# mLSTM cell in front of an MLP with a tanh-shrink, one core: the cell rebuilt with paired heads and a second part two slots behind its scores

## The chip, the core and the metric

The kernel runs on one core of a Trainium2 chip. The metric is the device time of one execution in microseconds (us), as the median of several runs. The core has five engines with an instruction queue each: PE (matrix multiplication, with its weight loads PEld), DVE (vector), ACT (scalar), POOL and SP, which here only issues DMAs. PE writes to PSUM, eight banks of 2 KB per partition; DVE and ACT read from it.

## What is computed

A recurrent cell over 4 batches, 8 heads, 768 tokens and 40 features per head, and behind it a dense part over all 3072 tokens (320 features, 2048 hidden). All of it in fp32.

```python
for t in range(S):
    m_new = np.maximum(f_gate[:, :, t] + m, i_gate[:, :, t])
    f_stab = np.exp(f_gate[:, :, t] + m - m_new)
    i_stab = np.exp(i_gate[:, :, t] - m_new)
    C = f_stab * C + i_stab * outer(vt, kt)      # 40 x 40 per head
    n = f_stab * n + i_stab * kt
    y[:, :, t] = sigmoid(o_gate) * (C @ qt) / np.maximum(np.abs(n @ qt), 1.0)
x = y, tokens by heads * features
h = x @ w_in
out = (h - np.tanh(h)) @ w_out
```

The weights arrive as 64-bit floats and are converted to fp32 in the kernel.

## The kernel before

**Cell.** The tokens are cut into 24 units of 128 tokens: unit n is chunk c = n // 4 of batch b = n % 4. Within a unit the recurrence is a product with a 128 x 128 decay matrix E per head, which one DVE scan (L321) makes from the gate's rows; across chunks a state of 40 x 41 per head goes on (the 41st column is n). A unit has these parts. `load_unit` (L132) issues five loads on SP's queue. `cell_open` (L311) issues the loads of E and qg, the scan on DVE, and on POOL the products qg (L324), vw (L326, L327) and vs (L330). `scores` (L332) multiplies k and q head by head (tile ps), four heads to a PSUM bank, and DVE multiplies four heads of E with it (L344). `output` (L364) adds, per head, state times qg and E times vw into the tile ph; its `close` divides and gates: den on DVE (L389 to L391), o times den on POOL (L392), ys on DVE (L394). `carry` (L348) makes pc, eight products of k and vs, and adds it to the state on DVE (L358) after POOL has decayed the state (L357). `turn` (L398) transposes ys into px, and ACT copies it to xT (L408). The tiles ph, pc and px share the two PSUM banks of the pool ps_b; ps has the two banks of ps_a.

A slot k (`cell_slot`, L413) is the list of steps: load unit k + 1, scores of the first four heads of unit k, turn of unit k - 2, output of unit k - 1, scores of the last four heads of unit k, carry of unit k - 1.

**Dense part.** Two units make a group of 256 tokens, twelve groups in all. An item is one group with one of eight pairs of 128-row blocks of the hidden layer: `up` (L433) makes 128 x 2 x 256 values in ph_up with 6 products, ACT and DVE compute h - tanh(h) from it in nine operations (L451 to L459) to the tile gt, and `down` (L463) adds 4 products into po, two items later. Each fp32 product of the program stands as two MATMUL instructions with a weight load each in the trace.

**Weights.** `weights` (L233) fetches a block as 64-bit integers and takes it apart on DVE (L255, L258), ACT (L256, L259, L260), POOL (L261, L262) and DVE again (`sign`, L266). `convert` strings blocks together so that each step fetches one block, computes the magnitude of another and the sign of a third.

**Order.** PE's instructions run in the order in which they are emitted (each hangs on the last, L75). The other engines' queues are ordered by a scheduler at compile time, which may draw ready instructions forward: the scans of units 16 to 18 start at 254.8, 267.3 and 298.0 us, before their slots. Slots 0 to 3 run ahead of the dense part, mixed with the conversion of pairs 0 and 1. The first six groups then go through the pairs in three passes (0 and 1; 2 to 4; 5 to 7), since the weights of later pairs are converted meanwhile; the other six groups go through all eight pairs. Slots 4 to 15 are spread over the twelve items of the first pass, one to an item; the last ten slots over the items from the second of the third pass on. Within an item `merge` (L492) alternates dense steps and cell steps by their written costs:

```python
            i = int(done[1] / total[1] < done[0] / total[0])
            if at[i] == len((a, b)[i]):
                i = 1 - i
            cost, step = (a, b)[i][at[i]]
            done[i] += cost
            at[i] += 1
            step()
```

Of the kernel before, what the change touches and what calls it, by code (L numbers as in the profile page):

```python
# [28 lines left out]
FP = mybir.dt.float32  # L30
# [22 lines left out]
def kernel(  # L53
# [71 lines left out]
    qk = [{name: const.tile([128, H, L], FP, name=f"{name}{i}") for name in ("qT", "kT")} for i in range(2)]  # L125
    for pair in qk:
        for name in pair:
            V.memset(pair[name], 0.0)
# [17 lines left out]
    ones = const.tile([128, D], FP, name="ones")  # L146
    diag = const.tile([128, H, L], FP, name="diag")
# [18 lines left out]
    eT = const.tile([D, NT, BH], FP, name="eT")  # L166
# [18 lines left out]
    for dst, w in ((eS, after), (eT, ones)):  # L185
        p = ps_b.tile([dst.shape[0], NT, BH], FP, name="psum_lf", tag="b")
        T.matmul(p.rearrange("p c n -> p (c n)"), w, lfT.rearrange("p c n -> p (c n)"),
                 start=True, stop=True)
        A.activation(out=dst, in_=p, func=AF.Exp)
# [32 lines left out]
    def spread(dst, rows, c, b):  # L222
        i, r = divmod((c * B + b) * H, NR)
        nc.sync.dma_start(out=dst, in_=rows[i:i + 1, r:r + H, :].to_broadcast([dst.shape[0], H, L]))
# [8 lines left out]
    def weights(dst, src):  # L233
# [4 lines left out]
        def fetch():  # L238
# [3 lines left out]
            w["st"] = conv.tile([128, n], I64, name="w64", tag="w64", bufs=4)[0:p]  # L242
            nc.sync.dma_start(out=w["st"], in_=src)

        def magnitude():
# [6 lines left out]
            r = w["r"] = conv.tile([128, n], I32, name="w_r", tag="w_r", bufs=3)[0:p]  # L252
# [20 lines left out]
    def convert(pairs):  # L273
# [9 lines left out]
        for x in range(len(blocks) + 3):  # L283
            def step(x=x):
                for late, part in enumerate((0, None, 1, 2)):
# [9 lines left out]
    qg = [const.tile([128, H, L], FP, name=f"qg{i}") for i in range(2)]  # L295
    ys = [const.tile([L, NK * 128], FP, name=f"ys{i}") for i in range(2)]
    state = [const.tile([128, H, D1], FP, name=f"state{b}") for b in range(B)]
    for i in range(2):
        G.memset(qg[i], 0.0)
        G.memset(ys[i], 0.0)  # L300
    for b in range(B):
        G.memset(state[b], 0.0)

# [4 lines left out]
    def per_token(t, w, k):  # L308
        return w[:, t["c"], t["hs"]].unsqueeze(2).to_broadcast([w.shape[0], H, k])

    def cell_open(n):  # L311
        c, b = divmod(n, B)
        t = un[n] = ld.pop(n)
        t["c"], t["b"], t["hs"] = c, b, slice(b * H, (b + 1) * H)
        E = t["E"] = att.tile([L, H, L], FP, name="E", tag="E", bufs=4)
        spread(E, f_rows, c, b)
        if c:
            t["qg"] = qg[n % 2]
            spread(t["qg"][0:D], g_rows, c, b)
        row = E.rearrange("p h t -> p (h t)")  # L320
        V.tensor_tensor_scan(out=row, data0=row, data1=diag.rearrange("p h t -> p (h t)"), initial=0.0,  # L321
                             op0=OP.mult, op1=OP.add)
        if c:
            G.tensor_tensor(out=t["qg"][0:D], in0=t["qg"][0:D], in1=t["qT"][0:D], op=OP.mult)  # L324
        vw = t["vw"] = att.tile([L, H, D1], FP, name="vw", tag="vw")
        G.tensor_tensor(out=vw[:, :, 0:D], in0=t["v"], in1=per_token(t, eiT, D), op=OP.mult)  # L326
        G.tensor_copy(out=vw[:, :, D], in_=eiT[:, c, t["hs"]])  # L327
        if c + 1 < NT:
            t["vs"] = att.tile([L, H, D1], FP, name="vs", tag="vs")
            G.tensor_tensor(out=t["vs"], in0=vw, in1=per_token(t, eS, D1), op=OP.mult)  # L330
# [256 lines left out]
```

## Time and profile before

| what | value |
|---|---|
| median of 3 runs (lowest, highest) | 742.69 us (741.7, 745.46) |
| the profiled execution | 744.64 us, span of the profile 742.9 us |
| PE, PEld busy | 668.3 us (90%), 542.9 us (73%) |
| DVE, ACT, POOL busy | 533.2 us (72%), 303.0 us (41%), 211.1 us (28%) |
| mean granted clock of PE | 0.924 |
| read from HBM, written | 46.20 MB, 4.13 MB |

The profile is of one execution. Busy is the time in which an engine ran instructions; a busy PE may run at half its clock. The granted clock is the share of full speed (2.4 GHz) that PE was given; it has two levels, 1.0 and 0.5, and a mean between them says how long each held. A row of the timeline or of the groups names line, engine, operation and "tile written <- tiles read"; brackets and the part behind a bar tell how long the engine idled before, and what ended that.

### The profile page before, as it was taken

What the parts mean: (1) busy time and instruction counts of PE and PEld (TensorE: products, weight loads), DVE (VectorE), ACT (ScalarE), POOL (GpSimd) and SP (SyncE); (2) the same over time, 40 slices, a digit from 0 to 9 for tenths busy, and PEclk for the clock granted to TensorE, in tenths of its full rate; (3) what the DMA queues carried; (4) which work ended last, traced back from release to release, by engine and by line L of the source; (5) the groups of instructions that cost most, each with busy time, mean ns of one, the idle gap of its engine ahead of it and who ended that gap; (6) DMA issues with size and microseconds to landing.
All of it is one profiled execution on the core that took longest, in us unless ns stands there. A gap on an engine that the chain in (4) does not pass through costs nothing.

```text
span 742.9 us, 9560 instructions
## 1 busy us (share of the span) xinstructions
PE 668.3 (90%) x3418; PEld 542.9 (73%) x3418; DVE 533.2 (72%) x845; ACT 303.0 (41%) x582; POOL 211.1 (28%) x226
## 2 busy tenths in 40 slices
PE   2477579898989977899999999999999999999997
PEld 1466468787877855678887877777778888877885
DVE  8775875786857898987768676766766665666665
ACT  3331332433422556644434343433354434544453
POOL 6385464644746456500021202020202020000000
PEclk9685896977869988999999999999999999999999
DMA  6562524444324612100011212120200100000000
GB/s 178 175 181 84 146 90 135 134 137 124 100 83 123 192 66 74 33 1 0 1 61 56 83 36 91 54 73 1 91 0 21 35 10 18 1 14 5 2 19 18
DMA packets 26487, 50.95 MB, mean 69 GB/s; under 512 B 3304, under 2 KB 15976, under 8 KB 26440
## 3 DMA queue, kind: packets, MB, share of 16 engines
q1 hardware_dynamic: 22568, 46.21, 20.0%
q10 hardware_dynamic: 3872, 4.13, 1.6%
q8 instruction: 27, 0.44, 0.2%
q14 instruction: 20, 0.16, 0.1%
HBM read 46.20 MB, written 4.13 MB: 68 GB/s over the span
## 4 chain that ended last, share of the span: by engine, by line
PE 67%; DVE 16%; POOL 9%; issue 5%; ACT 2%; ACTq 0%; DVEq 0%; POOLq 0%
PE ph_up L83 30%; PE po L83 23%; PE ph L83 8%; PE ps L83 4%; DVE E L321 3%; POOL w_r L261 3%; POOL w_r L262 2%; DVE gt L458 2%; PE pc L83 2%; DVE gt L457 2%; DVE gt L459 1%; POOL o L392 1%; DVE gt L455 1%; DVE t L456 1%; DVE w_e L255 1%
## 5 line engine op out<-in xcount | busy, mean ns | idle before, releaser
L83 PE MATMUL ph_up<-xT,w_in 128*128 128x256 f32 x1152 | 310.7, 397 | 0.0
L83 PE MATMUL po<-w_out,gt 128*128 128x320 f32 x768 | 253.5, 456 | 13.0 <-DVE part L477 6.6
L83 PEld LDWEIGHTS ph_up<-xT,w_in 128*128 128x128 f32 x1152 | 209.8, 195 | 32.4 <-issue 0.6
L83 PEld LDWEIGHTS po<-w_out,gt 128*128 128x128 f32 x768 | 140.9, 197 | 54.4 <-DVE part L477 8.7
L451 ACT ACTIVATE z<-ph_up 128x512 f32<-128x512 f32 x96 | 57.1, 595 | 263.4 <-PE ph_up L83 255.6
L455 DVE SCALAR_TENSOR_TENSOR gt<-ph_up,z 128x512 f32<-128x512 f32 x96 | 65.8, 685 | 98.6 <-ACT t L452 98.3
L83 PE MATMUL ps<-qT,kT 128*128 128x128 f32 x384 | 71.3, 313 | 27.2 <-DVE E L344 27.2
L83 PEld LDWEIGHTS ps<-qT,kT 128*128 128x128 f32 x384 | 68.0, 224 | 37.9 <-DVE E L344 28.6
L459 DVE COPY_PREDICATED gt<-big,t 128x512 f32<-128x512 int32 x96 | 81.3, 847 | 6.2
L83 PE MATMUL ph<-vw,E 128*128 128x41 f32 x384 | 80.2, 311 | 0.0
L457 DVE SCALAR_TENSOR_TENSOR gt<-z,gt 128x512 f32<-128x512 f32 x96 | 79.0, 823 | 0.0
L83 PEld LDWEIGHTS ph<-state,qg 128*128 128x128 f32 x320 | 64.9, 214 | 17.9 <-issue 7.4
L458 DVE SCALAR_TENSOR_TENSOR gt<-q,gt 128x512 f32<-128x512 f32 x96 | 72.1, 751 | 5.5
L453 ACT ACTIVATE q<-z,square 128x512 f32<-128x512 f32 x96 | 69.3, 722 | 0.0
L454 ACT ACTIVATE big<-z,border 128x512 f32<-128x512 f32 x96 | 69.1, 720 | 0.0
L357 POOL TENSOR_TENSOR state<-state,eT 40x328 f32<-40x328 f32 x16 | 11.9, 744 | 194.1 <-PE ph L83 194.1
L83 PEld LDWEIGHTS ph<-vw,E 128*128 128x128 f32 x384 | 66.1, 223 | 0.4 <-issue 0.2
L456 DVE TENSOR_TENSOR t<-ph_up,t 128x512 f32<-128x512 f32 x96 | 65.2, 679 | 0.0
L83 PE MATMUL ph<-state,qg 128*128 128x41 f32 x320 | 58.3, 268 | 5.6 <-DVE state L358 5.5
L261 POOL TENSOR_TENSOR w_r<-w_r,w_m 128x256 f32<-128x256 f32 (+2 forms) x40 | 39.1, 978 | 71.4 <-ACT w_m L259 65.7
L321 DVE TENSOR_TENSOR_SCAN E<-E,diag 128x1024 f32<-128x1024 f32 x24 | 59.0, 2456 | 0.0
L452 ACT ACTIVATE t<-ph_up 128x512 f32<-128x512 f32 x96 | 56.8, 592 | 0.0
(82 smaller groups left out, 488.4 us busy)
## 6 DMA issues: line engine op xcount, KB each, us to landing
E<-f_rows SPq DMA_DIRECT2D x24, 512.0 KB
w<-in_moe_w_out SPq DMA_DIRECT2D x16, 320.0 KB
w<-in_moe_w_in SPq DMA_DIRECT2D x16, 256.0 KB
qT<-in_qT SPq DMA_DIRECT2D x24, 160.0 KB
kT<-in_kT SPq DMA_DIRECT2D x24, 160.0 KB
v<-in_v SPq DMA_DIRECT2D x24, 160.0 KB
k<-in_k SPq DMA_DIRECT2D x24, 160.0 KB
o<-in_o_gate SPq DMA_DIRECT2D x24, 160.0 KB
```

The source lines that it names most:

```text
L83: return cls.keep(nc.tensor.matmul(*args, **kwargs))
L261: G.tensor_tensor(out=rf, in0=rf, in1=mf, op=OP.add)
L321: V.tensor_tensor_scan(out=row, data0=row, data1=diag.rearrange("p h t -> p (h t)"), initial=0.0, op0=OP.mult, op1=OP.add)
L451: A.activation(out=z, in_=ph, func=AF.Square)
L452: A.activation(out=t, in_=ph, func=AF.Tanh)
L453: A.activation(out=q, in_=z, func=AF.Square, bias=square)
L454: A.activation(out=big, in_=z, func=AF.Relu, bias=border)
L455: V.scalar_tensor_tensor(out=gt, in0=ph, scalar=lead, in1=z, op0=OP.mult, op1=OP.mult)
L456: V.tensor_tensor(out=t, in0=ph, in1=t, op=OP.subtract)
L457: V.scalar_tensor_tensor(out=gt, in0=z, scalar=root, in1=gt, op0=OP.add, op1=OP.mult)
L458: V.scalar_tensor_tensor(out=gt, in0=q, scalar=rest, in1=gt, op0=OP.add, op1=OP.mult)
L459: V.copy_predicated(gt, big.bitcast(I32), t)
```

## The change

The cell is written anew. Heads h and h + 4 form a pair. q2 holds both heads of a pair in one column block, the first at partitions 0 to 39, the second at 64 to 103; kz holds k the same way with zeros in the other half, so that a score still takes one product per head. The state of a pair is block-diagonal (104 partitions, 2 x 41 columns), so one product of qg and state serves two heads (`inter`), and so does one product of kp and vs (`update`), of which only the diagonal blocks are used. Each batch has two sets of states, and POOL writes the decayed old set into the new one. v1 carries a column of ones, so that vw and vs are one product each, vs with the factor eiS made once.

`fetch` loads unit s + 1 and its E in slot s; `decay` issues qg's loads and the scan of unit s; `prepare` runs POOL's products and the sigmoid of unit s - 1. The output of a unit is two slots behind its scores, its turn three, and within a slot scores, inter, intra and update alternate. The multiplication of o by den moves from POOL to DVE (`gate`). There are 27 slots: 0 to 3 ahead of the dense part, 4 to 16 in the first pass, 17 to 26 later, up to four items earlier than before. The conversion has one step more between magnitude and sign, and a buffer more for each of its two tiles.

```diff
--- before.py
+++ after.py
-    qk = [{name: const.tile([128, H, L], FP, name=f"{name}{i}") for name in ("qT", "kT")} for i in range(2)]
...
+    SEC = 64
+    TOP = SEC + D
+    kz = [const.tile([128, H, L], FP, name=f"kz{i}") for i in range(2)]
+    q2 = [const.tile([128, HH, L], FP, name=f"q2{i}") for i in range(2)]
+    kp = [const.tile([L, HH, TOP], FP, name=f"kp{i}") for i in range(4)]
+    v1 = [const.tile([L, H, D1], FP, name=f"v1{i}") for i in range(3)]
...
     def load_unit(n):
         c, b = divmod(n, B)
-        t = ld[n] = dict(qk[n % 2])
-        for name, src in (("qT", qT), ("kT", kT)):
-            nc.sync.dma_start(out=t[name][0:D], in_=src[b, c])
-        for name, src, bufs in (("v", v, 2), ("k", k, 3), ("o", o_gate, 3)):
-            t[name] = load.tile([L, H, D], FP, name=name, tag=name, bufs=bufs)
-            nc.sync.dma_start(out=t[name], in_=src[b, c])
+        t = ld[n] = {"kz": kz[n % 2], "q2": q2[n % 2], "kp": kp[n % 4], "v1": v1[n % 3]}
+        for half, (r0, h0) in enumerate(((0, 0), (SEC, HH))):
+            heads = slice(h0, h0 + HH)
+            nc.sync.dma_start(out=t["kz"][r0:r0 + D, heads], in_=kT[b, c, :, heads])
+            nc.sync.dma_start(out=t["q2"][r0:r0 + D], in_=qT[b, c, :, heads])
+        nc.sync.dma_start(out=t["v1"][:, :, 0:D], in_=v[b, c])
+        for r0, h0 in ((0, 0), (SEC, HH)):
+            nc.sync.dma_start(out=t["kp"][:, :, r0:r0 + D], in_=k[b, c, :, h0:h0 + HH])
+        t["o"] = load.tile([L, H, D], FP, name="o", tag="o", bufs=4)
+        nc.sync.dma_start(out=t["o"], in_=o_gate[b, c])
...
-    diag = const.tile([128, H, L], FP, name="diag")
+    diag = const.tile([128, H, L], BF, name="diag")
...
+    V.tensor_tensor(out=eiS, in0=eiT, in1=eS, op=OP.mult)
...
-            w["st"] = conv.tile([128, n], I64, name="w64", tag="w64", bufs=4)[0:p]
+            w["st"] = conv.tile([128, n], I64, name="w64", tag="w64", bufs=5)[0:p]
...
-            r = w["r"] = conv.tile([128, n], I32, name="w_r", tag="w_r", bufs=3)[0:p]
+            r = w["r"] = conv.tile([128, n], I32, name="w_r", tag="w_r", bufs=4)[0:p]
...
-                for late, part in enumerate((0, None, 1, 2)):
+                for late, part in enumerate((0, None, 1, None, 2)):
...
+    qg = [const.tile([128, HH, L], FP, name=f"qg{i}") for i in range(3)]
     ys = [const.tile([L, NK * 128], FP, name=f"ys{i}") for i in range(2)]
-    state = [const.tile([128, H, D1], FP, name=f"state{b}") for b in range(B)]
...
+    state = [[const.tile([128, HH, 2, D1], FP, name=f"state{b}_{i}") for i in range(2)] for b in range(B)]
+    for t in xT + qg + ys + sum(state, []):
+        G.memset(t, 0.0)
...
+    def fetch(n):
+        load_unit(n)
+        t = ld[n]
+        t["E"] = att.tile([L, H, L], FP, name="E", tag="E", bufs=4)
+        spread(t["E"], f_rows, n, 0)
+
+    def decay(n):
         t = un[n] = ld.pop(n)
...
+        if t["c"]:
+            t["qg"] = qg[n % 3]
+            for r0, h0 in ((0, 0), (SEC, HH)):
+                spread(t["qg"][r0:r0 + D], g_rows, n, h0)
+        row = t["E"].rearrange("p h t -> p (h t)")
         V.tensor_tensor_scan(out=row, data0=row, data1=diag.rearrange("p h t -> p (h t)"), initial=0.0,
                              op0=OP.mult, op1=OP.add)
...
+        t["vw"] = att.tile([L, H, D1], FP, name="vw", tag="vw", bufs=3)
+        G.tensor_tensor(out=t["vw"], in0=t["v1"], in1=per_token(eiT), op=OP.mult)
+        if t["c"]:
+            G.tensor_tensor(out=t["qg"][0:TOP], in0=t["qg"][0:TOP], in1=t["q2"][0:TOP], op=OP.mult)
+        if t["c"] + 1 < NT:
+            t["vs"] = att.tile([L, H, D1], FP, name="vs", tag="vs", bufs=3)
+            G.tensor_tensor(out=t["vs"], in0=t["v1"], in1=per_token(eiS), op=OP.mult)
...
+                G.tensor_tensor(out=new, in0=old, in1=eT[:, n, :].unsqueeze(2).to_broadcast([TOP, HH, 2 * D1]),
+                                op=OP.mult)
+        A.activation(out=t["o"], in_=t["o"], func=AF.Sigmoid)
...
+        T.matmul(t["ps"][:, h % HH, :], t["kz"][:, h, :], t["q2"][:, h % HH, :], start=True, stop=True)
...
+            T.matmul(pair(t["ph"], j), t["qg"][:, j, :], state[t["b"]][t["c"] % 2][:, j], start=(j == 0), stop=False,
+                     skip_group_check=True)
...
+        V.tensor_tensor(out=sg, in0=sg, in1=den.unsqueeze(2).to_broadcast([L, H, D]), op=OP.mult)
...
+        T.matmul(t["pc"][:, j], t["kp"][:, j, :], pair(t["vs"], j), start=True, stop=True)
...
+        for i, r0 in enumerate((0, SEC)):
+            new, pc = st[r0:r0 + D, :, i, :], t["pc"][r0:r0 + D, :, i, :]
+            if t["c"]:
+                V.tensor_tensor(out=new, in0=new, in1=pc, op=OP.add)
...
+    def cell_slot(s, o, x):
...
+        def begin():
+            if o is not None:
+                prepare(o)
+            if s is not None and s - 1 in un:
+                prepare(s - 1)
+            if s is not None:
+                if s + 1 < NU:
+                    fetch(s + 1)
+                decay(s)
+
+        steps.append((0.0, begin))
+        for d in range(HH):
+            for i in range(2):
+                if s is not None:
+                    steps.append((0.22, lambda h=2 * d + i: score(s, h)))
+                if o is not None and i == 0:
+                    steps.append((0.22 if o >= B else 0.0, lambda d=d: inter(o, d)))
+            if o is not None:
+                steps += [(0.22, lambda h=h: intra(o, h)) for h in (d, d + HH)]
+                if d in (1, 2) and o + B < NU:
+                    steps += [(0.18, lambda j=j: update(o, j)) for j in (2 * d - 2, 2 * d - 1)]
+        if o is not None:
+            steps.append((0.0, lambda: gate(o)))
+        if x is not None:
+            steps += [(0.11, lambda j=j: turn(x, j)) for j in range(NK)]
...
+    slots = [(0, None, None), (1, 0, None), (2, 1, 0), (3, None, 1)]
+    AHEAD = len(slots)
+    slots += [tuple(n if lo <= n < NU else None for n, lo in ((s, 0), (s - 2, 2), (s - 3, 2)))
+              for s in range(AHEAD, NU + 3)]
...
+    def slots_for(g):
+
+        return AHEAD if g == 0 else GT * g + 5
...
-    x0, x1 = starts[1, PASSES[-1][0]], starts[NG - 1, 0]
...
+    x0, x1 = starts[1, PASSES[-1][0]], starts[NG - 1, 0] - HH
```

## Rows read from the trace of the kernel before

**Rows 1.** Stages: stretch, its us; busy by engine; PEclk, DMA share, GB/s.

```profile
52.35:250.06 197.71, 166.90 (x1014) 143.59 (x1013) 141.10 (x212) 62.73 (x134) 103.83 (x108) 0.79 0.40 122
250.06:367.43 117.37, 106.10 (x423) 82.47 (x421) 98.14 (x163) 64.78 (x129) 37.74 (x33) 0.94 0.13 43
367.43:666.79 299.36, 298.02 (x1505) 237.34 (x1503) 204.92 (x320) 121.80 (x219) 37.86 (x38) 1.00 0.12 39
```

**Rows 2.** Same view, single items of the first pass.

```profile
192.17:203.54 11.37, 11.37 (x89) 10.10 (x87) 8.95 (x16) 5.89 (x13) 6.39 (x8) 1.00 0.42 131
203.54:226.41 22.87, 19.32 (x88) 16.31 (x87) 13.81 (x21) 4.51 (x9) 11.74 (x13) 0.63 0.24 76
```

**Rows 3.** Timeline of one slow item: start, us, engine, line [idle before].

```profile
201.55 2.35 POOL L324 TENSOR_TENSOR qg<-qg,qT 40x1024 f32<-40x1024 f32 x1
...
201.70 2.75 DVE L457 SCALAR_TENSOR_TENSOR gt<-z,gt 128x512 f32<-128x512 f32 x1
...
207.14 0.49 DVE L394 TENSOR_TENSOR ys<-ph,o 128x320 f32<-128x320 f32 x1 [1.43 <-POOL o L392]
...
207.78 0.52 PE L87 MATMUL px<-ident,ys 128*128 128x128 f32 x3 [2.32 <-DVE ys L394]
```

**Rows 4.** Waits from 52 to 250 us: total, times, longest.

```profile
DVE den L389 <- PE ph L83: 33.0, 9, 7.0
...
PE ps L83 <- DVE E L344: 16.9, 3, 9.0
...
DVE w_out L266 <- POOL w_r L262: 8.4, 7, 2.4
...
DVE ys L394 <- POOL o L392: 6.6, 9, 1.4
```

**Rows 5.** Timeline of warm small matmuls, then two pieces of the chain.

```profile
75.93 0.30 PEld L83 LDWEIGHTS ph<-state,qg 128*128 128x128 f32 x2
...
76.38 0.30 PEld L83 LDWEIGHTS ph<-state,qg 128*128 128x128 f32 x2
...
79.47 0.97 PEld L83 LDWEIGHTS ps<-qT,kT 128*128 128x128 f32 x8
...
81.00 0.81 PE L83 MATMUL pc<-vs,k 128*40 128x41 f32 x16
...
320.16 2.59 PE ph_up L83 x12
...
322.75 2.15 PE po L83 x8
```

**Rows 6.** Groups from 52 to 250 us: busy us, mean ns | idle.

```profile
L321 DVE TENSOR_TENSOR_SCAN E<-E,diag 128x1024 f32<-128x1024 f32 x13 | 33.9, 2606 | 0.0
...
L457 DVE SCALAR_TENSOR_TENSOR gt<-z,gt 128x512 f32<-128x512 f32 x12 | 17.3, 1441 | 0.0
...
L456 DVE TENSOR_TENSOR t<-ph_up,t 128x512 f32<-128x512 f32 x12 | 8.1, 679 | 0.0
...
L394 DVE TENSOR_TENSOR ys<-ph,o 128x320 f32<-128x320 f32 x12 | 5.9, 488 | 6.6 <-POOL o L392 6.6
...
L324 POOL TENSOR_TENSOR qg<-qg,qT 40x1024 f32<-40x1024 f32 x12 | 29.1, 2422 | 3.9 <-DMA qg<-g_rows 3.9
...
L392 POOL TENSOR_TENSOR o<-o,den 128x320 f32<-128x320 f32 x12 | 10.5, 878 | 3.8 <-DVE den L391 3.8
```

**Rows 7.** DMA queues (packets, MB, share), and one issue by SP.

```profile
q1 hardware_dynamic: 22568, 46.21, 20.0%
q10 hardware_dynamic: 3872, 4.13, 1.6%
175.65 0.38 SPq L139 DMA_DIRECT2D v<-in_v  x1
```

**Rows 8.** POOL: a memset's group, and the first conversion's row.

```profile
L231 POOL MEMSET w_in<- 128x2048 f32 x1 | 1.8, 1804 | 0.0
...
21.01 0.72 POOL L261 TENSOR_TENSOR w_r<-w_r,w_m 128x256 f32<-128x256 f32 x1 [5.67 <-ACT w_r L260]
```

More of the change, by code (lines that the diff above doesn't have):

```diff
@@ L122 @@
     nc.sync.dma_start(out=i_sb, in_=i_gate)
-    qk = [{name: const.tile([128, H, L], FP, name=f"{name}{i}") for name in ("qT", "kT")} for i in range(2)]
-    for pair in qk:
-        for name in pair:
-            V.memset(pair[name], 0.0)
+    SEC = 64
[4 more added lines that the diff above has]
+    v1 = [const.tile([L, H, D1], FP, name=f"v1{i}") for i in range(3)]
+    for i in range(4):
+        if i < 2:
+            V.memset(kz[i], 0.0)
+            V.memset(q2[i], 0.0)
+        V.memset(kp[i][:, :, D:SEC], 0.0)
+        if i < 3:
+            V.memset(v1[i][:, :, D:D1], 1.0)
     ld = {}
@@ L332, in scores @@
-    def scores(n, half):
-        h4 = slice(half * HH, (half + 1) * HH)
-        def product(j):
-            if j == 0 and half == 0:
-                cell_open(n)
-            t = un[n]
-            if j == 0:
-                t["ps"] = ps_a.tile([L, HH, L], FP, name="ps", tag="a")
-            h = half * HH + j
-            T.matmul(t["ps"][:, j, :], t["kT"][:, h, :], t["qT"][:, h, :], start=True, stop=True)
-            if j == HH - 1:
-                V.tensor_tensor(out=t["E"][:, h4, :], in0=t["ps"], in1=t["E"][:, h4, :], op=OP.mult)
-        return [(0.22, lambda j=j: product(j)) for j in range(HH)]
@@ L348, in carry @@
-    def carry(n):
-        def update(h):
-            t = un[n]
-            st = state[t["b"]]
-            if h == 0:
-                t["pc"] = ps_b.tile([D, H, D1], FP, name="pc", tag="b")
-            T.matmul(t["pc"][:, h, :], t["k"][:, h, :], t["vs"][:, h, :], start=True, stop=True)
-            if h == H - 1:
-                if t["c"]:
-                    G.tensor_tensor(out=st[0:D], in0=st[0:D], in1=per_token(t, eT, D1), op=OP.mult)
-                    V.tensor_tensor(out=st[0:D], in0=st[0:D], in1=t["pc"], op=OP.add)
-                else:
-                    V.tensor_copy(out=st[0:D], in_=t["pc"])
-        return [(0.08, lambda h=h: update(h)) for h in range(H)] if n // B + 1 < NT else []
@@ new lines, in intra, with gate @@
+    def intra(n, h):
+        t = un[n]
+        T.matmul(t["ph"][:, h, :], t["E"][:, h, :], t["vw"][:, h, :], start=(t["c"] == 0 and h == 0), stop=True,
+                 skip_group_check=True)
+    def gate(n):
+        t = un[n]
+        ph, sg = t["ph"], t["o"]
+        den = att.tile([L, H], FP, name="den", tag="den")
+        V.tensor_scalar(out=den, in0=ph[:, :, D], scalar1=-1.0, scalar2=1.0, op0=OP.mult, op1=OP.max)
+        V.tensor_tensor(out=den, in0=den, in1=ph[:, :, D], op=OP.max)
+        V.reciprocal(out=den, in_=den)
+        V.tensor_tensor(out=sg, in0=sg, in1=den.unsqueeze(2).to_broadcast([L, H, D]), op=OP.mult)
+        y = t["y"] = ys[n % 2]
+        V.tensor_tensor(out=y[:, 0:DM].rearrange("p (h d) -> p h d", d=D), in0=ph[:, :, 0:D], in1=sg, op=OP.mult)
```

163 lines of the change are left out of this document (69 added, 94 removed).

## The prediction, written before the changed kernel had been run

> **What bounds the kernel now.** Four views, in this order. The stage table first [rows 1]: after a prologue, the stretch from 52 to 250 us, in which twelve items of the dense part carry twelve cell slots, has a granted clock of 0.79, PE busy 84% and DVE busy 71%. Nothing is full there. From 250 to 367 us DVE is busy 84% (weights are still converted), and from 367 to 667 us PE is busy 99.6% at clock 1.00: that stage is bound by PE's instructions and by nothing else.
>
> Then the same stretch cut at the first matmul of each item [rows 2]. The twelve rows fall into two kinds, and one of each stands there: six of 9.2 to 12.2 us with clock 1.00 (mean 11.4) and six of 18.8 to 23.4 us with clock 0.59 to 0.77 (mean 21.6). A slow item does the same work; its PE is cold and idle. So 6 x 10.2 = 61 us of the 198 us are the price of the slow items.
>
> Third, one slow item's start in the timeline [rows 3]. POOL multiplies qg for 2.35 us; DVE's L457, issued 0.15 us later, takes 2.75 us and ends 0.55 us after POOL; ys waits 1.43 us for POOL's o; PE's transposes wait 2.32 us for ys, because px, ph and pc share two PSUM banks. After the stall follows the output phase, 32 matmuls of 41 columns. That item is the slow one of [rows 2], clock 0.63.
>
> Fourth, the waits of the stretch [rows 4]: DVE waits 33.0 us at den for PE's ph, and 15.0 us for POOL (w_out 8.4, ys 6.6); PE waits 16.9 us for the decay product E.
>
> **PE's instructions, part by part.** Warm, two small matmuls of ph follow two others every 0.22 us (the pair of state at 75.93, that of vw, the next of state at 76.38), so one costs 0.11 us [rows 5]; it is not the 41 columns, since pc has as many on 40-column weights at 0.05; a score costs the same (8 in 0.97 us, 0.12). What counts is the number of 128-column weight loads. The dense item costs 2.59 + 2.15 = 4.74 us [rows 5].
> - State times qg: 16 instructions per unit become 8 of 82 columns, still bound by the load: -8 x 0.11 = -0.88 us for each of 20 units.
> - pc: 16 in 0.81 us [rows 5], 0.05 each with 40-column weights; now 8 with 104-column weights. Bounds 0.05 and 0.11 each, so 0.4 to 0.9 us; nearest to 128 columns, I take 0.09, 0.7 us: no change.
> - Scores, the product with vw and the transposes keep their counts. Alternating the kinds buys nothing by itself, since 0.11 is the price in a run of one kind and in a mixture.
> - One slot more lies in the first pass (slots 4 to 16, thirteen, were 4 to 15), one fewer behind: its scores, 16 x 0.11 = 1.8 us of PE, move forward.
>
> **DVE, POOL, ACT, SP.** DVE's 141.1 us in the stretch [rows 1] change thus. The gating of sg comes over from POOL: nearest is ys, same shape, 0.49 us [rows 6], 13 times, +6.4. The state's addition is split by partitions: 679 ns for 512 columns and 488 for 320 [rows 6] give 1 ns a column, so 0.50 us for 328 and 2 x 0.33 for twice 164, +0.16 x 11 = +1.8. The slot moved forward brings a scan and two products of 512 columns, 2.6 + 2 x 0.68 = +4.0. The bf16 diag I price at nothing (bounds: nothing, or half of each scan, -17 us; the count of elements is unchanged). Blocking: L457 costs 1441 ns against 679 for L456 of the same shape, 9.1 us in the stretch, and the scan 2606 [rows 6]. POOL's work falls by half of qg's 2.42 us (half the columns) and by o's 0.88 [rows 6], 2.1 us a unit, 25 of the 104 us of [rows 1]; I take a third off those 9.1, -3 (bounds 0 and -9). Together 150.3 us, 12.5 per item; PE warm needs 4.74 + 13/12 x 40 x 0.11 + 0.8 + 0.4 = 10.7. So with no wait at all DVE becomes the bound of this stretch, at 150 us.
>
> Sigmoid only moves earlier on ACT, which is busy 62.7 us of 198 [rows 1]: nothing. POOL's memsets grow by some 6,200 columns, 5.5 us at w_in's 1.80 us for 2048; POOL idles 5.67 us before its first w_r [rows 8]: covered, and without that cover the first weights would be late by them. The conversion's last step comes one step later with one more buffer: DVE's 8.4 us of waits for w_r [rows 4] should go.
>
> SP issues 11 loads a unit for 7, at 0.38 us [rows 7] 4.2 us plus about 0.6 for weights; if an issue grows with its runs (1024 for v, 512 twice for k, against 128), 3.0 + 3.0 + 8 x 0.38 + 0.6 = 9.6 us. Both stay under 12.5. E, so far issued in the slot that scans it, is now issued one slot ahead, behind q2 and kz, which wait for POOL's qg of the unit before: a late POOL would hold E, then the scan, then the scores' bank; a slot of slack lies between.
>
> The data engines: v and k arrive in 2048 runs of 160 bytes a unit instead of 256 of 1280. The trace has no such run. Below, the bytes are the same: nothing. Above, the packets of the output queue (1067 bytes on average) took 0.016 x 16 x 742.9 / 3872 = 49 ns, those of the load queue (2048 bytes) 105 ns [rows 7]; at 49 ns each engine gets 128 x 0.049 - 1.0 = +5.3 us a unit on 0.40 x 198 / 12 = 6.6 us an item [rows 1], 12.3: just hidden. I take it as hidden. The Trainium skill (DMA: Bandwidth & Descriptors, Specifications) speaks against this part: under 512 bytes a transfer is read, modified and written, below line rate. By that, counted as two passes of the 49 ns, an item would have 19 us of transfers and the sum would come to 759 us, an estimate; no run here shows such a transfer.
>
> **The sum.** First stretch: 150.3 plus what remains of waiting. The 15.0 us for POOL go; of the 33.0 us at den, which come from six cold output phases, I keep those of two to three cold items, 14 us. That is 164 for 198: -34 (bounds 150 and 198). Prologue: unit 2's output leaves it, 16 x 0.12 + 0.8, -3 (bounds +3, should E come late, and -6). 250 to 367 us: DVE-bound with the same work and less blocking, -3 (0 to -8). Then nine outputs at -0.8 each (one load in ten lies behind a dense matmul) and the slot's scores -1.8: -9 (0, if stalls eat it, to -10). Sum -49. The profiled execution took 744.64 us (span 742.9), 2 us above the median of 742.69; against the median 742.7 - 49 = 694.
>
> **The rivals.**
> - *The banks hold it.* ph, pc and px still share two banks, and gate is now five DVE operations at the end of the slot, in front of the next ph. If the next ph waits for it each time, that is 1.5 us (three operations of 8 columns at 0.18 by the same line, two of 0.49) and up to a whole scan of 2.6 us in front [rows 6], PE stalls as in [rows 3], and the items stay mixed at 198 / 12 = 16.5 us. Then only prologue, conversions and half of the last stage remain: 742.7 - 3 - 1 - 4 = 735. For it: px waits just so in [rows 3]. Against: gate has lost its hop over POOL, and pc's bank comes free mid-slot.
> - *All items warm.* Nothing stalls PE for long, the small matmuls lie between scores and dense ones, and DVE's 150 us stand: 694 - 14 = 680; with the better bounds of the other stages 671.
> - *Slower: the short runs bound the slot.* If a run of 160 bytes costs what a 2048-byte packet does, 105 ns, an engine gets 128 x 0.105 - 1.0 = +12.4 us a unit, 13/12 of that on 6.6 is 20 us an item, 241 in the stretch: +43, less 15 elsewhere, 771. It costs from 59 ns on (where an item passes 13.7 us) and turns the gain into a loss near 88. Against it: 49 ns for far larger packets.
> - *The clock does not follow the order.* Falls come from stalls alone and the interleaving changes nothing: between forecast and first rival, 710; its chance is within the forecast's.
>
> **How the numbers follow.** Forecast 0.60, all warm 0.18, banks 0.12, short runs 0.07, anything else 0.03. A measurement can tell about 0.5%, 3.7 us. Faster takes the first two and two thirds of the banks: 0.86; same 0.06; slower 0.08. The range goes from 662 (all warm with the bounds of prologue, conversion and perhaps a faster scan) to 732, close to the banks' case; it leaves out the short runs and about half of the banks.
>
> **What would show it.** Item by item, the stretch should have two or three items over 16 us in place of six, a clock near 0.93, and DVE busy above 85% of it; no wait of ys or w_out for POOL; L457 nearer 1.1 us; state instructions 160 for 320; the late stage full at clock 1.00 and 8 to 10 us shorter. Wrong, if PE waits for ys or gate in most slots, if the transfers' share passes 0.8, or if the scan waits for E.

## The result, and the profile after

The changed kernel takes 708.01 us (median of four runs, 705.85 to 709.64) against 744.08 for the kernel before on the same chip (741.7 to 746.6): a ratio of 0.951, 95% interval 0.947 to 0.956. Forecast were 694, with a range of 662 to 732. So it is faster, as expected, but by 36 us in place of 49, and three of the forecast's four stages came out far from it. The profiled execution after has a span of 706.6 us. The stage table, cut at the same places as [rows 1] (the first matmul of items 0, 12, 33 and 82):

```profile
0.00:60.98 60.98, 28.02 (x137) 26.76 (x137) 46.62 (x89) 17.35 (x36) 33.14 (x54) 0.72 0.59 159
60.98:238.62 177.64, 145.35 (x869) 127.71 (x870) 142.40 (x238) 62.80 (x136) 81.34 (x88) 0.87 0.51 142
238.62:354.80 116.18, 104.37 (x423) 80.94 (x422) 101.14 (x168) 67.25 (x134) 35.36 (x34) 0.96 0.14 39
354.80:631.15 276.35, 276.35 (x1378) 228.84 (x1377) 202.03 (x332) 120.81 (x217) 14.61 (x15) 1.00 0.13 38
```

| stretch | before, us | after, us | forecast | came |
|---|---|---|---|---|
| up to the first dense item | 52.35 | 60.98 | -3 | **+8.6** |
| first pass, 12 items | 197.7 | 177.6 | -34 | **-20.1** |
| conversions | 117.4 | 116.2 | -3 | -1.2 |
| late stage | 299.4 | 276.4 | -9 | **-23.0** |
| rest | 76.1 | 75.5 | 0 | -0.6 |
| sum | 742.9 | 706.6 | -49 | -36.3 |

Three rows of the same view for single items answer to [rows 2]. The two kinds are gone: the twelve items last 11.8 to 18.8 us, 14.8 on average, and a shorter item can have a lower mean clock than a longer one (0.87 beside 0.95).

```profile
106.68:121.02 14.34, 10.23 (x58) 8.85 (x59) 10.95 (x22) 3.73 (x9) 7.15 (x8) 0.88 0.46 131
142.07:153.85 11.78, 11.78 (x73) 10.59 (x72) 10.42 (x18) 5.02 (x12) 4.80 (x6) 0.87 0.55 135
170.95:184.70 13.75, 11.40 (x73) 9.63 (x71) 11.01 (x19) 5.84 (x13) 6.24 (x7) 0.95 0.40 99
```

The waits of the first pass after the change (total, times, longest), which answer to [rows 4]:

```profile
POOL state L369 <- DVE state L420: 38.0, 7, 6.5
...
PE px L89 <- DVE state L420: 23.5, 7, 5.3
...
DVE w_out L291 <- POOL w_r L287: 12.1, 7, 1.9
...
DVE w_in L291 <- POOL w_r L287: 8.3, 8, 1.6
...
PE px L89 <- DVE state L422: 2.4, 1, 2.4
```

DVE's 33.0 us at den and its 6.6 at ys are gone. The waits for w_r, which were to go with them, are not: w_out has 12.1 us where it had 8.4, and w_in 8.3 where it had 7.8. And a wait has come that no row of before has: px, whose bank is the one that pc leaves, waits for the addition that reads pc. One such place in the timeline (it answers to [rows 3]): the addition's second half stands behind an instruction of the dense part in DVE's queue, and PE and POOL both go on 0.14 us after its end. That px is not held by ph's bank is seen from the gate, which begins to read ph only at 184.88 us.

```profile
182.19 0.31 DVE L420 TENSOR_TENSOR state<-state,pc 40x164 f32<-40x164 f32 x1
182.42 0.68 DVE L495 SCALAR_TENSOR_TENSOR gt<-q,gt 128x512 f32<-128x512 f32 x1
...
183.13 0.33 DVE L420 TENSOR_TENSOR state<-state,pc 40x164 f32<-40x164 f32 x1
...
183.60 1.19 POOL L369 TENSOR_TENSOR state<-state,eT 104x328 f32<-104x328 f32 x1 [6.40 <-DVE state L420]
183.60 0.52 PE L89 MATMUL px<-ident,ys 128*128 128x128 f32 x3 [2.32 <-DVE state L420]
```

The groups of the first pass (busy us, mean ns | idle), beside [rows 6]: the scan costs 2320 ns for 2606, what was L457 costs 728 for 1441, qg, with half the columns, 1470 for 2422, while a sign of w_out, behind POOL, costs 1207 for 891.

```profile
L348 DVE TENSOR_TENSOR_SCAN E<-E,diag 128x1024 f32<-128x1024 f32 x13 | 30.2, 2320 | 0.0
...
L363 POOL TENSOR_TENSOR qg<-qg,q 104x512 f32<-104x512 f32 x12 | 17.6, 1470 | 0.3 <-DMA qg<-g_rows 0.3
...
L291 DVE SCALAR_TENSOR_TENSOR w_out<-w,w_r 128x320 int32<-128x320 int32 x8 | 9.7, 1207 | 12.1 <-POOL w_r L287 12.1
...
L494 DVE SCALAR_TENSOR_TENSOR gt<-z,gt 128x512 f32<-128x512 f32 x12 | 8.7, 728 | 0.0
```

The load queue of [rows 7] now has three times the packets for the same bytes:

```profile
q1 hardware_dynamic: 69360, 46.22, 23.8%
```

### The profile page after: what moved, and what is told of

Read it like the earlier page. It is cut to its first block, busy times and chain, and to the rows that moved or that the text cites. A ratio compares the mean times of both kernels' runs of the same rounds, so it can differ in the third digit from the quotient of the medians.

```text
span 706.6 us, 9050 instructions
## 1 busy us (share of the span) xinstructions
PE 625.3 (89%) x3098; PEld 520.4 (74%) x3098; DVE 541.0 (77%) x897; ACT 303.4 (43%) x584; POOL 164.5 (23%) x190
## 4 chain that ended last, share of the span: by engine, by line
PE 69%; DVE 16%; POOL 5%; ACT 4%; issue 4%; DMA 2%; SPq 1%; ACTq 0%; POOLq 0%; DVEq 0%
PE ph_up L85 31%; PE po L85 25%; PE ps L85 5%; PE ph L85 5%; DVE E L348 3%; POOL w_r L286 2%; POOL w_r L287 2%; PE pc L85 1%; DVE gt L495 1%; DVE gt L494 1%; DVE gt L492 1%; DVE t L493 1%; DVE w_in L291 1%; PE px L89 1%; DVE E L380 1%
## 5 line engine op out<-in xcount | busy, mean ns | idle before, releaser
L85 PE MATMUL po<-w_out,gt 128*128 128x320 f32 x768 | 249.1, 449 | 10.7 <-DVE part L514 9.8
L85 PEld LDWEIGHTS po<-w_out,gt 128*128 128x128 f32 x768 | 138.8, 195 | 49.7 <-DVE part L514 12.1
L85 PE MATMUL ps<-q,kz 128*128 128x128 f32 x384 | 85.0, 323 | 17.5 <-DVE E L380 11.7
L85 PEld LDWEIGHTS ps<-q,kz 128*128 128x128 f32 x384 | 74.3, 228 | 25.8 <-DVE E L380 11.9
L496 DVE COPY_PREDICATED gt<-big,t 128x512 f32<-128x512 int32 x96 | 76.5, 796 | 6.5 <-DVE gt L495 0.5
L85 PEld LDWEIGHTS ph<-vw,E 128*128 128x128 f32 x384 | 69.4, 214 | 7.9
L494 DVE SCALAR_TENSOR_TENSOR gt<-z,gt 128x512 f32<-128x512 f32 x96 | 67.5, 703 | 0.0
L85 PE MATMUL ph<-vw,E 128*128 128x41 f32 x384 | 61.9, 267 | 0.0
L363 POOL TENSOR_TENSOR qg<-qg,q 104x512 f32<-104x512 f32 x20 | 28.2, 1410 | 117.4 <-DMA qg<-g_rows 90.1
L286 POOL TENSOR_TENSOR w_r<-w_r,w_m 128x256 f32<-128x256 f32 (+2 forms) x40 | 36.3, 907 | 56.2 <-ACT w_m L284 43.1
L366 POOL TENSOR_TENSOR vs<-v,eiS 128x328 f32<-128x328 f32 x20 | 17.7, 884 | 108.8 <-PE pc L85 108.8
L89 PE MATMUL px<-ident,ys 128*128 128x128 f32 x72 | 17.0, 305 | 26.5 <-DVE state L420 23.5
```

The source lines that it names most:

```text
L85: return cls.keep(nc.tensor.matmul(*args, **kwargs))
L286: G.tensor_tensor(out=rf, in0=rf, in1=mf, op=OP.add)
L494: V.scalar_tensor_tensor(out=gt, in0=z, scalar=root, in1=gt, op0=OP.add, op1=OP.mult)
L496: V.copy_predicated(gt, big.bitcast(I32), t)
```

## The late stage: what a narrow weight tile costs among wide ones

PE is full in this stage in both kernels, so every microsecond is PE's. Fitting the 49 items' times beyond 4.74 us by their counts of small instructions gives, before, 0.12 for a score, 0.11 for either half of ph, and **0.213** for pc; after, 0.11 for all and 0.102 for pc. So pc fell from 80 x 0.213 = 17.0 to 40 x 0.102 = 4.1 us, the state's products from 144 x 0.111 to 72 x 0.112 (-7.9), the scores by one slot's 16 (-2.7). These make up the 23 us, which is nearly two thirds of the whole gain. The forecast had the second and the third and took pc for unchanged. Two kernels part the width of pc's weights from their number.

**The kernel before, with wide weights (e3).** Its pc products load 80 columns, their own head and the next:

```
-            T.matmul(t["pc"][:, h, :], t["k"][:, h, :], t["vs"][:, h, :], ...)
+            T.matmul(t["pc"][:, h, :], t["k"][:, h:h + 2, :].rearrange("p two d -> p (two d)"), t["vs"][:, h, :], ...)
```

> The kernel before, with pc's weights 80 columns wide: each product loads its own head and the next one, and the lower 40 rows of the result alone are used. The instruction count stays 16 a unit. Theory (the width of the load relative to its neighbours is what costs): pc falls from 0.213 to about 0.11 us an instruction in the late stage, 80 x 0.1 = 8 us there (299.4 to some 291), the whole from 744 to about 735. Rival (only count and columns matter; 0.05 us in a run of pc goes up towards 0.11 with the wider load): the late stage is the same or longer by up to 5 us, the whole 744 to 749.

**The changed kernel, with narrow weights (e2).**

```
-        T.matmul(t["pc"][:, j], t["kp"][:, j, :], pair(t["vs"], j), ...)
+        for i, r0 in enumerate((0, SEC)):
+            T.matmul(t["pc"][r0:r0 + D, j, i, :], t["kp"][:, j, r0:r0 + D], t["vs"][:, j + i * HH, :], ...)
```

> pc goes back to one product per head on a 40-column weight tile (16 instructions a unit for 8), all else as after the change. Theory (a 40-column weight load among 128-column ones costs a switch): the late stage grows from 276.4 us by 80 x 0.213 - 40 x 0.102 = 13 us to some 289, the whole from 708 to 720 or more, and pc costs about 0.2 us an instruction there. Rival A (only the number of loads counts, 0.11 each): +4.4 us, 712. Rival B (the price read in a run of pc alone, 0.05 each): 80 x 0.05 - 40 x 0.102 = 0, no change.

Measured: e3's late stage is 291.5 us for 299.4 (-7.8), but of the whole only 2.5 us are gone, short of the expected 735, with a ratio to the kernel before of 0.996 (0.992 to 0.9995; in the profiled execution its first pass was 8 us longer, for a reason that was not sought); e2's late stage is 280.35 for 276.35 (+4.0), the whole 711.3 us, ratio 0.956 (0.950 to 0.962). The stage rows of e2 and of e3:

```profile
349.70:630.05 280.35, 280.35 (x1418) 226.21 (x1417) 201.93 (x332) 121.01 (x217) 15.08 (x15) 1.00 0.13 38
```

```profile
376.06:667.59 291.53, 289.75 (x1505) 240.27 (x1504) 205.15 (x320) 122.01 (x219) 37.15 (x38) 1.00 0.13 40
```

In the late stage e3 confirms that the width counts, while e2 hits the number of rival A, and read per instruction the two do not agree: in e2 a narrow pc costs 0.10, as a wide one does. The timelines bring them together. Call a visit the pc instructions that stand together between dense products. Before (first fence) and in e3 (second), pairs of pc alternate with pairs of po:

```profile
391.11 0.27 PE L83 MATMUL pc<-vs,k 128*40 128x41 f32 x2
391.31 0.81 PE L83 MATMUL po<-w_out,gt 128*128 128x320 f32 x2
392.05 0.27 PE L83 MATMUL pc<-vs,k 128*40 128x41 f32 x2
```

```profile
399.64 0.27 PE L83 MATMUL pc<-vs,kw 128*80 128x41 f32 x2
399.74 0.79 PE L83 MATMUL po<-w_out,gt 128*128 128x320 f32 x2
400.36 0.27 PE L83 MATMUL pc<-vs,kw 128*80 128x41 f32 x2
```

From one pc to the next it is 0.94 us with 40 columns and 0.72 with 80, and 40 such visits times 0.2 are e3's 8 us. In e2 (first fence) a visit is four narrow instructions long, after the change (second) two wide ones:

```profile
360.25 0.79 PE L85 MATMUL po<-w_out,gt 128*128 128x320 f32 x2
360.97 0.28 PE L85 MATMUL pc<-vs,kp 128*40 128x41 f32 x4
361.17 0.81 PE L85 MATMUL po<-w_out,gt 128*128 128x320 f32 x2
361.82 0.59 PE L85 MATMUL ph_up<-xT,w_in 128*128 128x256 f32 x2
```

```profile
365.35 0.79 PE L85 MATMUL po<-w_out,gt 128*128 128x320 f32 x2
365.98 0.33 PE L85 MATMUL pc<-vs,kp 128*104 128x82 f32 x2
366.14 0.74 PE L85 MATMUL po<-w_out,gt 128*128 128x320 f32 x2
366.72 0.59 PE L85 MATMUL ph_up<-xT,w_in 128*128 128x256 f32 x2
```

The same stretch, po to ph_up, takes 1.57 us and 1.37; 20 visits times 0.2 are e2's 4.0 us. Against two wide instructions in the same place, a visit of two narrow ones costs 0.2 us more, and a visit of four narrow ones costs 0.2 more too. So **the price is 0.2 us for each visit of 40-column weights among 128-column ones**, not for each instruction, and [rows 5] could not show it, since there the sixteen stand in one run. By this count some 8 of pc's 12.9 us are the 40 narrow visits, and the rest, about 4.5, the forty instructions fewer. The Trainium skill (TensorEngine Tiling (Array Packing), Key Properties) has a rule that the forecast did not use: changing the tiling mode of the array drains it, where another tile of the same mode does not. These runs agree with it only if a 40-column load runs in such a mode and an 80-column one does not, which no row says, so why a visit costs 0.2 us is not shown; the size is these runs' own.

## The first pass: a ring of waits

DVE is busy 142.4 of 177.6 us (80%), PE 82%; neither is full. Seven kernels change one thing each in the changed kernel; the last column is the ratio to the kernel before (the change itself: 0.951, 0.947 to 0.956).

| kernel | first item at | first pass | conversions end at | ratio |
|---|---|---|---|---|
| the change | 60.98 | 177.6 | 354.8 | 0.951 |
| e1, pc earlier | 60.7 | 187.7 | 369.5 | 0.971 (0.967 to 0.976) |
| f1, ph copied out by ACT | 60.0 | 174.2 | 349.3 | 0.945 (0.942 to 0.949) |
| k1, state's product kept back | 61.0 | 179.2 | 355.4 | 0.954 (0.950 to 0.958) |
| g1, no alternation | 58.2 | 182.8 | 358.5 | 0.958 (0.955 to 0.961) |
| g2, gate's product on POOL | 60.0 | 182.2 | 357.2 | 0.951 (0.948 to 0.955) |
| g3, one slot's distance | 66.96 | 155.9 | 345.9 | 0.944 (0.940 to 0.947) |
| s1, v and kp loaded twice | 57.75 | 174.9 | 348.7 | 0.947 (0.944 to 0.950) |

**e1: pc earlier.** If px waits for the state's addition, an earlier pc should free the bank in time.

```
-                if d in (1, 2) and o + B < NU:
-                    steps += [(0.18, lambda j=j: update(o, j)) for j in (2 * d - 2, 2 * d - 1)]
+                u = d - (o < AHEAD - 2)
+                if u in (0, 1) and o + B < NU:
+                    steps += [(0.18, lambda j=j: update(o, j)) for j in (2 * u, 2 * u + 1)]
```

> Only the place of pc changes: from the slots of the first pass on, its two groups come after d = 0 and d = 1 and no longer after d = 1 and d = 2, so that the state's addition is behind DVE a quarter of a slot earlier. Theory (px takes pc's bank and waits for the state's addition; POOL's state product of the next unit waits for the same addition and holds the weights' products behind it): PE's wait of px for the state's addition falls from 25.9 us in the first pass to under 8, POOL's wait of state for it from 41.4 us to under 25, the first pass from 177.6 us to 160 to 168, the whole from 708 to some 692 to 698 us. Rival (DVE, busy 80% of the stretch, is simply late, and the bank is only where that shows): px then waits for ys or the next ph for the addition, the first pass stays within 4 us of 177.6, the whole within 704 to 710.

It is 15 us slower than the change, and theory and rival both miss. The wait only moved, as its row shows: now pc comes third, and waits for the gate of the unit before, which holds the other bank.

```profile
PE pc L85 <- DVE ys L407: 23.5, 10, 5.2
```

**f1: ph copied out.** ACT copies ph to memory as soon as it is done, and the gate reads the copy.

```
-        ph, sg = t["ph"], t["o"]
+        ph, sg = att.tile([L, H, D1], FP, name="hb", tag="hb", bufs=1), t["o"]
+        A.copy(out=ph, in_=t["ph"])
```

> After the change, with one copy more: ACT copies ph out of its bank as soon as its last product is done (0.5 us by the copy of px, 0.48), and the gate reads the copy. Theory (three tiles share two banks, and whichever comes third waits for DVE, whose queue is some 4 us behind; the place of pc only chooses which): with ph's bank free within about a microsecond, px takes it; PE's waits for DVE's ys or state in the first pass fall from 25.9 us to under 8, the pass from 177.6 to 155 to 166 us, the whole from 708 to 690 to 698. Rival (DVE is the bound already, 142 us of work and 20 us of waits for POOL: PE's waits are only its lateness): PE waits elsewhere instead, for ps or E, the pass stays above 172 and the whole above 702.

The waits at the two banks fall to 7 us (px for DVE 4.9, px for ACT's copy 2.1), as the theory has it; the gain is the rival's, 3.5 us in the pass. DVE's lateness shows one step further on, where the scores wait for the products that empty their banks. DVE is now busy 147.9 of 174.2 us. The row of waits:

```profile
PE ps L85 <- DVE E L380: 18.2, 9, 4.2
```

**k1: the state's product kept back.** POOL's longest wait is for the state's product of a unit four further on, which the planner has put right behind the addition whose sum it reads. The weights' products stand behind it.

```
+            near = un.get(n + 1, t)
+            tc.add_manual_dep(product.ins, near.get("vs_op", t["vs_op"]).ins.name, NO_SYNC, ...)
```

> After the change, with POOL's state product of a unit kept behind its own neighbours: it may run only after vs of the next unit, where the planner had hoisted it to just behind the state's addition four units earlier (it reads what that addition writes). Theory (POOL's 38 us of waits for DVE's addition hold the weights' products in its queue; DVE then waits 20.4 us for w_r, a circle between two queues): POOL's wait of state falls under 8 us, DVE's waits for w_r from 20.4 to under 13, the first pass from 177.6 to 166 to 171 us, the whole to 697 to 703. Rival (DVE would idle anyway, for ACT or PE, at the pace of the two banks): the waits move, the pass stays above 174, the whole within 704 to 710.

POOL's wait for the addition went, and nothing was gained: POOL waits for ACT instead, ACT for DVE, and DVE for w_r as before:

```profile
POOL w_r L286 <- ACT w_m L284: 54.0, 11, 10.8
...
DVE w_out L291 <- POOL w_r L287: 12.3, 7, 2.4
...
DVE w_in L291 <- POOL w_r L287: 10.6, 8, 1.6
```

**g1: the alternation undone.** All eight scores of a slot stand ahead of the second part.

```
-        for d in range(HH):
-            for i in range(2):
-                if s is not None:
-                    steps.append((0.22, lambda h=2 * d + i: score(s, h)))
+        if s is not None:
+            steps += [(0.22, lambda h=h: score(s, h)) for h in range(H)]
+        for d in range(HH):
+            for i in range(2):
```

> After the change, with the alternation alone undone: in every slot the eight scores of one unit stand in a run, then the second part of the other unit, all else (pairs, two slots' distance, gate on DVE) as it is. Theory (alternation buys nothing by itself; what ended the cold output phases is the distance of two slots): the first pass stays within 5 us of 177.6, the late stage within 2 of 276.4, the whole within 703 to 713. Rival (a run of 41-column products lets PE's clock fall and scores in a run wait for ps banks): DVE's or PE's waits for ps and ph come back, the pass grows to 185 to 195 us with items over 18 us, the whole to 716 to 726.

The pass is 5.2 us longer, the whole 713.35: just outside the theory's band, well short of the rival's. No item is over 18.2 us, and the late stage is the same to 0.1 us. So the alternation is worth 5 us at most, and it is not what made the longest items shorter.

**g2: the gate's product back on POOL.**

```
-        V.tensor_tensor(out=sg, in0=sg, in1=den...)
+        G.tensor_tensor(out=sg, in0=sg, in1=den...)
```

> After the change, with the gate's product of o and den back on POOL, all else as it is. Theory (the first pass runs at the pace of DVE's queue, full to 80% and waiting for POOL in the rest; a hop over POOL in the middle of the gate makes ys, and with it the banks, later still): DVE's work falls by 13 x 0.55 = 7 us, DVE and PE wait longer for ys, the pass is 178 to 186 us, the whole 708 to 716. Rival (what is taken off DVE comes off the time): the pass falls by 5 to 8 us, the whole to 700 to 703.

DVE's work falls by 5.2 us and the pass grows by 4.6; the conversions end 2.4 us later, and the whole is the same (708.6), at the theory's lower edge. What is taken off DVE does not come off the time.

**g3: one slot's distance.** The second part is one slot behind the scores again, the turn two.

```
-    slots = [(0, None, None), (1, 0, None), (2, 1, 0), (3, None, 1)]
+    slots = [(0, None, None), (1, 0, None), (2, 1, 0), (3, 2, 1)]
...
-    slots += [... ((s, 0), (s - 2, 2), (s - 3, 2)) ... range(AHEAD, NU + 3)]
+    slots += [... ((s, 0), (s - 1, 3), (s - 2, 2)) ... range(AHEAD, NU + 2)]
...
-        return AHEAD if g == 0 else GT * g + 5
+        return AHEAD if g == 0 else GT * g + 4
```

> After the change, with the distance alone undone: the second part of a unit comes one slot behind its scores and the turn two, as in the kernel before; the alternation, the pairs and the gate on DVE stay. Theory (the distance is what removed the 33 us in which DVE waited at den for ph, and the cold items with it): PE waits for E at the start of the second part, the first pass grows to 185 to 197 us, the whole to 714 to 726; the late stage gets a second part more and a slot's scores, some 3 us. Rival (the distance is not needed; halved products, the gate and the alternation did it): the pass stays within 4 us of 177.6, the whole within 705 to 713.

Both miss, on the same side: it is faster by 5 us (702.7; the intervals just touch). The first pass carries one slot fewer and one output is ahead of it, so the end of the conversions is the fair mark: 345.9 against 354.8 us. The late stage takes 1.8 us of it back. No wait of DVE at den returns, and the wait at px is small. Its stages, then two of its waits in the first pass:

```profile
66.96:222.89 155.93, 133.53 (x829) 115.80 (x829) 131.04 (x226) 61.12 (x129) 75.53 (x82) 0.93 0.55 150
222.89:345.94 123.05, 107.09 (x423) 82.39 (x421) 101.11 (x169) 66.87 (x132) 35.69 (x35) 0.93 0.17 45
```

```profile
PE pc L85 <- DVE ys L407: 8.7, 5, 2.5
...
PE px L89 <- DVE state L420: 5.8, 7, 2.1
```

Together: four queues hand work round (PE to DVE for a bank, DVE to ACT to POOL and back for the weights), and freeing one link shows the next. What **stays open** is which part of the change took the 20 us off the pass. Undone alone, the distance is no gain, and without alternation or gate the pass is some 5 us longer; halving the state's products and qg was not undone alone, nor were two parts together. And 5 us are little here: s1 below and e2 only add work, and yet their conversions end 6.1 and 5.1 us earlier than the change's (348.7 and 349.7 for 354.8). So an edit can shift these stages by as much as f1, g1 and g2 did without touching what it is meant for, and their few us are not shown to be the price of the part.

**s1: the short runs.** v and kp are loaded twice into the same tiles.

```
-        nc.sync.dma_start(out=t["v1"][:, :, 0:D], in_=v[b, c])
-        for r0, h0 in ((0, 0), (SEC, HH)):
+        for _ in range(2):
+            nc.sync.dma_start(out=t["v1"][:, :, 0:D], in_=v[b, c])
+        for r0, h0 in 2 * ((0, 0), (SEC, HH)):
```

> After the change, with v and kp of every unit loaded twice: 2048 runs of 160 bytes and three issues of SP a unit more, into the same tiles. Theory (a packet of 160 bytes costs some 14 ns and is hidden): the queue's packets grow by about 49,000, the share of the data engines in the first pass from 0.51 to 0.60 to 0.66, the whole stays within 704 to 714 (SP issues 1.8 us a unit more). Rival (short runs hold the loads back already, and what the forecast called the short runs' price is part of the 8.5 us of the prologue and of the pass): the pass grows by over 10 us, the whole to 722 or more.

The whole is 705.7 us, no slower. The load queue (packets, MB, share), then the first pass in the stage table:

```profile
q1 hardware_dynamic: 119664, 54.09, 30.8%
```

```profile
57.75:232.64 174.89, 143.76 (x869) 126.08 (x870) 136.26 (x243) 64.13 (x136) 96.91 (x91) 0.87 0.66 164
```

50,304 packets more took 0.308 x 16 x 701.7 - 0.238 x 16 x 706.6 = 767 us of the sixteen engines, 15 ns each: not 49, not 105. With 1.7 times the packets the transfers' share of the first pass rises from 0.51 to 0.66, and no time is lost.

## The prologue: 8.6 us lost, and part of it got back elsewhere

Scores after the change start again at 34.52 us (31.53 before), and from there to the first item it is 26.5 us (20.8 before). Two kernels try the two halves.

**e4: scores in a run ahead of the first item.**

```
+        lead = o is not None and o < AHEAD - 2
+        if lead and s is not None:
+            steps += [(0.22, lambda h=h: score(s, h)) for h in range(H)]
...
-                if s is not None:
+                if s is not None and not lead:
```

> In the slots ahead of the first dense item the eight scores of a unit stand in one run again, ahead of the second part of the other unit, as in the kernel before; the later slots alternate as after the change. Theory (with the kinds alternating, PE's clock stays at 0.50 up to the first item, where the runs of scores had brought it to 1.00 from 44 us on): the granted clock of 44 to 54 us rises from 0.50 above 0.8 and the first item starts at 54 to 57 us in place of 60.8, the whole at 702 to 705. Rival (the prologue ends when the weights and ys are through DVE, whose conversions come late because their loads were issued late): the clock may rise, but the first item starts within 1 us of 60.8 and the whole stays within 706 to 710.

The rival holds for the prologue: the clock of 44 to 54 us rises to 0.67, the first item comes 0.6 us earlier. The whole, 704.95 us, lies in the theory's band, but its ratio of 0.9475 (0.942 to 0.953) is not to be told from that of the change.

**e5: the first 30 us.** Three edits: only the padding of xT and ys is set to zero, unit 0's sigmoid waits for the last exponential, unit 1 is loaded ahead of E(0).

```
-    for t in xT + qg + ys + sum(state, []):
-        G.memset(t, 0.0)
+    for t in qg + sum(state, []):
+        G.memset(t, 0.0)
+    for t in xT:
+        G.memset(t[:, NK - 1, :], 0.0)
...
+        if n == 0:
+            tc.add_manual_dep(sig.ins, last_exp.ins.name, NO_SYNC, ...)
...
+    load_unit(1)
     spread(ld[0].setdefault("E", ...), f_rows, 0, 0)
```

> After the change, with three edits of the first 30 us: only the padding of xT and ys is set to zero, not the whole tiles; the first sigmoid waits for the last exponential, so that two table loads of 1.28 us go; and SP issues unit 1's loads ahead of the first E. Theory (the prologue is 8.5 us longer because f_rows come 1.5 us later, E(0) is scanned 1.9 us later, and SP is then held until 31 us by loads in short runs, so that weights and unit 2 come late): the first scan starts at 28 to 29 us in place of 30.3, the first item at 54 to 58 us in place of 60.8, the whole at 702 to 705. Rival (what is lost is lost after 34 us, in PE's half clock and the wait of 4 us for ys): the scan comes earlier, the first item gains under 2 us, the whole stays within 706 to 709.

The theory holds: first item at 56.2 us, the whole 702.3, ratio 0.943 (0.939 to 0.947). The rows of xr and of the first scan, after the change (first fence) and in e5 (second):

```profile
10.48 3.46 DVE L218 TENSOR_SCALAR xr<-lfT 128x192 f32<-128x192 f32 x1
...
30.25 2.81 DVE L348 TENSOR_TENSOR_SCAN E<-E,diag 128x1024 f32<-128x1024 f32 x1
```

```profile
10.47 0.26 DVE L218 TENSOR_SCALAR xr<-lfT 128x192 f32<-128x192 f32 x1
...
26.19 2.28 DVE L353 TENSOR_TENSOR_SCAN E<-E,diag 128x1024 f32<-128x1024 f32 x1
```

While POOL zeroed its tiles, one DVE instruction of 0.26 us took 3.46. With the three edits, the scan comes 4.1 us earlier and the scores 5.2 (29.32, which is 2.2 us earlier than before the change). What each of the three is worth was not parted. The other half stays: from there to the first item it is 26.8 us in e5, 6 us more than before the change, and why stays open.

**The three that gained, together (h5):** e5's start, one slot's distance, ph copied out.

> Three edits on the kernel after the change at once: the start of the prologue, the distance of one slot, and ph copied out by ACT. Theory (they act in different places: 5.5 us before the first item, some 10 us less between first item and the end of the conversions, 3.5 us from the banks): the first item starts near 59 us (its slots hold one output more), the conversions end at 335 to 342 us in place of 354.6, the late stage is 278, the whole 690 to 697. Rival (with one slot's distance PE waits only 14 us for banks, and DVE's order is what paces both): the copy buys nothing or costs ACT's time, the conversions end at 342 to 347, the whole 697 to 702.

699.5 us, ratio 0.938 (0.935 to 0.941): faster than the change by 8.5 us and the fastest here, but in the rival's band. The start keeps its gain (58.99 for g3's 66.96); the conversions end at 345.84, where g3 alone has 345.94. So what the start and the copy save is lost again before the conversions end.

## Where the forecast was right and wrong

- **The whole** came inside the range and on the forecast side, but in part by luck, with errors that partly cancel: -14 on the late stage, +11.6 on the prologue, +14 on the first pass.
- **pc, "no change"**, is the step that failed in the late stage. Its price was read from a run of sixteen; among dense products it is 17.0 us before and 4.1 after. Bounds of 0.05 and 0.11 did not hold the 0.213. The state's products (-7.9) and the scores (-2.7) came near the reckoning (-7.2 and -1.8).
- **The prologue, -3 with a bound of +3**, failed in sign. "POOL idles 5.67 us before its first w_r: covered" counted POOL's own time and not what its memsets do to DVE (3.46 for 0.26) or the order of ACT and SP behind it. Adding memsets beyond the cover was named as the risk, but priced at nothing. Of the 8.6 us, 3.0 lie ahead of the first scores; the 5.6 behind them stay open.
- **"The 15.0 us for POOL go"**: those at ys did, those for w_r grew, as did the signs' own time (w_out 1207 ns for 891). The waits of w_in, 7.8 us before and 8.3 after, were not in the sum. One step later in the program did not help, since POOL reaches w_r late through ACT and DVE themselves (k1).
- **DVE as the bound, 150.3 us**: it has 142.4. L457's blocking fell by 713 ns an instruction, 8.6 us and not 3 (the bound was 9), and the scan's by 286. The bf16 diag gained nothing by itself: an unblocked scan takes 2.28 us in both kernels. DVE is not full, and the 35 us above it are the ring of waits, where the sum had 14 us of cold items. The prediction's own signs for this stage failed too: four items are over 16 us, the clock is 0.87 for 0.93, DVE is busy 80% and not over 85%.
- **The banks' rival** named the mechanism, a tile that waits for DVE because three share two banks, but the late link was the state's addition, not the gate; its price (198 us for the pass) was too high.
- **The 33.0 us at den**, of which the sum kept 14, are gone, but not by the two slots' distance: with one slot they do not return (g3).
- **Short runs hidden**: right, with a far lower price than the bounds. The rule of the Trainium skill (DMA: Bandwidth & Descriptors, Specifications), by which the estimate of 759 us was made, has no trace here: 15 ns for a packet of 160 bytes leaves no room for a second pass of 49.

## What to carry to other kernels

Read an instruction's price in the mixture in which it will run: a run of sixteen hid 0.2 us per visit. Where two banks serve three tiles in turn, moving one of them moves the wait (e1); look for what makes the emptying engine late before buying distance or copies. Price the work that is added to an idle engine by whom it blocks, not by its own time.

## What the runs showed that was not expected

- 40-column weights between 128-column products: 0.2 us a visit, whether two instructions long or four; 80 and 104 columns: none of it.
- A DVE tensor_scalar of 192 columns took 3.46 us during POOL's memsets, 0.26 without.
- The clock column can mislead at the start of a trace. In e5 it has 1.00 for 34 to 44 us, and yet four scores take 1.20 us, as they do after the change at 0.50; at 61.04 us they take 0.65, and the column has 1.00 there too. In e5's trace the first entry of the clock is a rise to 1.00 at 59.9 us, and the column counts the time before a first entry as 1.00. So PE was most likely at the lower level until then, and a clock without an entry is read by a product whose price is known. Stage table and timeline, e5:

```profile
34.00:44.00 10.00, 7.17 (x36) 7.02 (x34) 6.91 (x15) 3.25 (x8) 3.19 (x4) 1.00 0.61 179
```

```profile
37.55 1.20 PE L85 MATMUL ps<-q,kz 128*128 128x128 f32 x4
...
61.04 0.65 PE L85 MATMUL ps<-q,kz 128*128 128x128 f32 x4
```

The same two views after the change:

```profile
34.00:44.00 10.00, 9.48 (x46) 9.49 (x47) 6.30 (x9) 0.49 (x1) 1.19 (x2) 0.50 0.45 154
```

```profile
42.75 1.20 PE L85 MATMUL ps<-q,kz 128*128 128x128 f32 x4
```
